# A grouped-query attention block with cached K and V: wo in longer rows, a second P buffer, a later P*V and an earlier K

## The chip, the cores and the metric

The kernel runs on one core of one Trainium2 chip. The core has five engines with queues of their own: PE (TensorE, matmuls; the trace also shows its weight loads as PEld), DVE (VectorE), ACT (ScalarE), POOL (GpSimd) and SP (SyncE, which issues nearly all transfers here). Sixteen DMA engines move data between HBM and the on-chip memory SBUF. Matmul results go to PSUM, 8 banks of 512 f32 on each of 128 partitions. The metric is the device time in microseconds of one execution; lower is better.

## The reference

32 batches, 4 query positions each, model width 1024, 32 query heads in 4 groups that share a K and V head, a cache of 2048 positions, head size 128, all bf16.

```python
q = (x @ wq).reshape(B, Sq, Hq, Dh).transpose(0, 2, 1, 3)
k = jnp.repeat(k_cache, rep, axis=1)
v = jnp.repeat(v_cache, rep, axis=1)
scores = jnp.einsum("bhqd,bhkd->bhqk", q, k) * (Dh ** -0.5)
p = softmax(scores)
o = jnp.einsum("bhqk,bhkd->bhqd", p, v)
return o.transpose(0, 2, 1, 3).reshape(B, Sq, Hq * Dh) @ wo
```

K and V of one batch are 2 MB each, wq and wo 8 MB each: some 151 MB are read once.

## The kernel before

The program is written by hand as five in-order queues. `p.op(engine, emit, waits, done)` appends an instruction with the events that it waits for; `p.dma` does the same for a transfer. Nothing reorders the queues.

**Loads.** `big` is a ring of 8 slots of 2 MB (16 KB on each of 128 partitions). First wq takes four of them; then K and V of each batch follow one another in the list `loads`: K is three batches ahead (`LEAD = 3`), so the order is K0, K1, K2, K3, V0, K4, V1 and so on, and at the end K31, V28, V29, V30, V31. SP issues them in this order (L171). Load n takes the slot of load n-8 and waits until that one has been used: a K until its four transposes are done (`("kt", b, 3)`), a V until its P*V is done (`("pv", b)`). One row of a K or V load is the 16 KB of a partition. After the last V, wo goes into the four slots that come next, in ten pieces (`WO`: seven of four heads or 1 MB, one of two, two of one head), with one row of 2 KB for each head and partition (L183).

**One batch**, i, goes through these steps:
- `kt`: DVE transposes K in four chunks of 16 positions in 32x32 blocks (L269) into one of two `KT_sb` buffers.
- `qd`: POOL lays the batch's queries out as a block diagonal over the four groups (L260), so that one matmul does all groups.
- `pe_qk`: 16 matmuls of 512 columns write the scores to `ps_s`, four PSUM banks (L281 and, with the weights held, L16). They wait for the exp of the batch before, which reads the same banks.
- `softmax_max` (DVE, L289, L290), `softmax_exp` (ACT, L294, with the sums) into `P_sb`.
- `pt`: DVE transposes P into one of two `PT_sb` (L302); `pd`: POOL copies it, group by group, into the block diagonal `PD_sb` (L314, four copies), which was cleared once. `PD_sb` is a single buffer: the copies wait for the P*V before. Batch 30 uses a second one, `PE_sb`, which is laid over a free `KT_sb` and cleared by ACT in iteration 30 (L378). Of the last batch's four copies DVE does three.
- `pe_pv`: 64 matmuls of P with V (L321) into one of four PSUM banks that are used in turn (`slot`).
- `o_evac`: ACT scales by the inverse sum into `o_sb` (L328); `pe_ot`: PE transposes it with an identity (L334); `ot_evac`: ACT writes it to `oT_sb` (L338), which is laid over `QT_sb` with the heads innermost. `o_evac` of a batch waits for the transpose of the one before, since `o_sb` is single.

**The order in iteration i** on each queue: queries i+1, half of K's transposes i+1, scores i, max i, output transpose i-3, exp i, the other half of K's transposes i+1, P's transpose i, P*V i-2 with `o_evac`, and the copies `pd` of i-1. So P*V is two batches behind the scores. After the loop come the last two P*V and what belongs to them.

**The end.** `oproj` (L349, L16) does 32 heads times two matmuls of 512 columns, each head with the wo rows of that head as moving operand and `oT_sb[:, :, h]` as weights, all into one accumulation. It waits for the last `ot_evac` and, piece by piece, for wo. Then DVE (L357) and ACT (L358) take half of the result each to `y_sb`, and SP and ACT store it (L360).

Of the kernel before, what the change touches and what calls it, by code (L numbers as in the profile page):

```python
# [78 lines left out]
def bass_standalone__gqa_block_cached__sampling_kernel(  # L79
# [21 lines left out]
    NW = 4  # L101
    LEAD = 3
    NC = D // 2
    WO = (4, 4, 4, 4, 4, 4, 4, 2, 1, 1)
# [5 lines left out]
    with ExitStack() as es:  # L110
# [8 lines left out]
        QT_sb = sbuf("QT_sb", [128, B, 2, REP, Sq, 2], BF16)  # L119
        oT_sb = QT_sb[:, :, :, :, :, :].rearrange("p b a h s w -> p (b a h s w)").rearrange("p (t h) -> p t h", h=Hq)  # L120
        QD_sb = sbuf("QD_sb", [128, 2, 2, G, 32, 2], BF16)
# [5 lines left out]
        PD_sb = sbuf("PD_sb", [128, T // 2, G, 32, 2], BF16)  # L127
        PE_sb = KT_sb[:, B % 2, :, :, :, :].rearrange("p t a r w -> p (t a r w)")
        PE_sb = PE_sb.rearrange("p (t g q w) -> p t g q w", t=T // 2, g=G, q=32)
        o_sb = sbuf("o_sb", [128, Dh], BF16)  # L130
        y_sb = sbuf("y_sb", [128, D], BF16)

# [27 lines left out]
        for b in range(B):  # L160
            loads += [("k", b + LEAD)] if b + LEAD < B else []
            loads += [("v", b)]
        slot_of = {}
        holder = {s: "w" for s in range(NW)}
        for n, (kind, b) in enumerate(loads):
            s = (NW + n) % NS
            before, holder[s], slot_of[kind, b] = holder.get(s), (kind, b), s
            waits = [] if before is None else ["qproj"] if before == "w" else [
                ("kt", before[1], NCH - 1) if before[0] == "k" else ("pv", before[1])]
            src = (k_cache if kind == "k" else v_cache)[b].rearrange("g (r t) d -> (g r) t d", r=R)  # L170
            p.dma("sp", lambda e, s=s, src=src: e.dma_start(big[:, s, :, :], src), waits, (kind, b), f"s_b{s}")  # L171
        n = len(loads)
        wo_slot = [(NW + n + c) % NS for c in range(NW)]

        def wo_at(h):
            return big[:, wo_slot[h // 8], :, :].rearrange("p t d -> p (t d)")[:, h % 8 * D:(h % 8 + 1) * D]

        h0 = 0
        for c, m in enumerate(WO):
            assert h0 // 8 == (h0 + m - 1) // 8  # L180
            kind, b = holder[wo_slot[h0 // 8]]
            dst = big[:, wo_slot[h0 // 8], :, :].rearrange("p t d -> p (t d)")[:, h0 % 8 * D:(h0 % 8 + m) * D]
            p.dma("sp", lambda e, dst=dst, h0=h0, m=m: e.dma_start(  # L183
                dst.rearrange("p (h n) -> p h n", h=m), wo[h0 * 128:(h0 + m) * 128, :].rearrange("(h p) n -> p h n", p=128)),
                [("kt", b, NCH - 1) if kind == "k" else ("pv", b)], ("wo", c), f"s_wo{c}")
            h0 += m
# [64 lines left out]

        ring_of = {}

        def qd(i):
# [50 lines left out]
        def pd_of(i):  # L305
            return PE_sb if i == B - 2 else PD_sb

        def pd(i):
            for g in range(G):
                rows = slice(32 * g, 32 * (g + 1))  # L310
                src = words(PT_sb[rows, i % 2, :, :, :].rearrange("p t q w -> p t (q w)"))
                dst = words(pd_of(i)[rows, :, g, :, :].rearrange("p t q w -> p t (q w)"))
                waits = [("pt", i)] + (["pe0"] if i == B - 2 else ["pd0"] + ([("pv", i - 2 if i == B - 1 else i - 1)] if i else []))
                p.op("dve" if i == B - 1 and g < 3 else "pool", lambda e, s=src, d=dst: e.tensor_copy(d, s),  # L314
                     waits, ("pd", i, g))

        def pe_pv(i):
            buf, waits = slot(("o", i))
            ring_of["o", i] = buf
            for t in range(T):  # L320
                p.op("pe", lambda e, t=t: e.matmul(  # L321
                    buf[:, 0:Dh], lhsT=pd_of(i)[:, t // 2, :, :, t % 2].rearrange("p g q -> p (g q)"),
                    rhs=big[:, slot_of["v", i], t, :], start=(t == 0), stop=(t == T - 1)),
                    waits + [("pd", i, g) for g in range(G)] + [("v", i)] if t == 0 else [], ("pv", i) if t == T - 1 else None)

# [5 lines left out]
        def pe_ot(i):  # L331
            buf, waits = slot(("ot", i))
            buf = ring_of["ot", i] = buf.bitcast(BF16)
            p.op("pe", lambda e: e.transpose(buf[:, 0:128], o_sb[:, :], ident[:, :]), waits + [("o", i)], ("oT", i))  # L334

        def ot_evac(i):
            buf = ring_of["ot", i]
            p.op("act", lambda e: e.activation(  # L338
                oT_sb[:, i * Sq:(i + 1) * Sq, :].rearrange("p s h -> p h s"),
                buf[:, 0:128].rearrange("p (h s) -> p h s", s=Sq), ACT.Copy),  # L340
                [("oT", i), ("qd", i)], ("ot", i))


        def oproj(c):
            for h in range(sum(WO[:c]), sum(WO[:c + 1])):
                for j in range(2):
                    out_, lhsT, rhs = ps_s[:, NC * j:NC * (j + 1)], oT_sb[:, :, h], wo_at(h)[:, NC * j:NC * (j + 1)]
                    if j == 0:
                        mm = lambda e, a=(out_, lhsT, rhs), h=h: e.matmul(  # L349
                            a[0], lhsT=a[1], rhs=a[2], start=(h == 0), stop=(h == Hq - 1), skip_group_check=True)  # L350
                    else:
                        mm = lambda e, a=(out_, lhsT, rhs), h=h: _matmul_held(
                            nc, e, *a, tile_size=(128, 128), tile_position=(0, 0), start=(h == 0), stop=(h == Hq - 1))
                    p.op("pe", mm, [("wo", c), ("ot", B - 1), ("exp", B - 1)], ("op", j) if h == Hq - 1 else None)
# [8 lines left out]
        L = B - 1  # L363
        p.at["qt_all"] = p.at["qt", 3]
        qd(0)
        kt(0, range(NCH))
        for i in range(B):
            if i < L:
                qd(i + 1)
                kt(i + 1, (0, 1))  # L370
            pe_qk(i)
            softmax_max(i)
            if i >= 3:
                pe_ot(i - 3)
                ot_evac(i - 3)
            softmax_exp(i)
            if i == L - 1:
                p.op("act", lambda e: e.memzero(words(PE_sb.rearrange("p t g q w -> p (t g q w)"))), [("qk", i)], "pe0")  # L378
            if i < L:
                kt(i + 1, (2, 3))  # L380
            pt(i)
            if i >= 2:
                pe_pv(i - 2)
                o_evac(i - 2)
            if i >= 1:
                pd(i - 1)

        pe_pv(L - 1)
        pe_ot(L - 2)
        ot_evac(L - 2)  # L390
        o_evac(L - 1)
        pd(L)
        pe_pv(L)
        pe_ot(L - 1)
        ot_evac(L - 1)
        o_evac(L)
        pe_ot(L)
# [60 lines left out]
```

## Time and profile before

| what | value |
|---|---|
| median of 5 runs | 369.34 us (369.09 to 370.71) |
| profiled execution, its own time | 369.41 us |
| its span | 367.6 us |
| PE busy | 280.5 us (76%) |
| DVE busy | 275.3 us (75%) |
| ACT busy | 123.2 us (34%) |
| POOL busy | 164.7 us (45%) |
| moved by the DMA engines | 151.90 MB, mean 413 GB/s |
| SP's loads and stores, share of 16 engines' span | 97.9% |

The span runs from the first to the last recorded instruction; the time of the execution is longer by what lies around it. Busy shares are means over stages. A slice is a fortieth of the span, 9.19 us, counted from 0 here. In lists of instructions L321 is line 321 of the kernel; "x64" means that many instructions merged; the brackets behind a line give the idle time before it on its engine and who ended it. A PE instruction is pitched closer to the next than its own duration, since matmuls are pipelined.

### The profile page before, as it was taken

To read this page: it belongs to the slowest core of one execution; us is meant where nothing else is said; L and a number is where in the kernel's file an instruction comes from. 1 tells how busy PE (TensorE), PEld (TensorE's weight loads), DVE (VectorE), ACT (ScalarE), POOL (GpSimd) and SP (SyncE) were. 2 spreads that over 40 slices of the span, in tenths; PEclk is the share of its full clock that TensorE was granted. 3 is DMA by queue.
4 is the path that set the end of the run, shared out by engine and by line. 5 is a ranking of instruction groups with operands and counts; after the bars stand their busy time and mean duration, and the time that the engine had idled before them with its cause. 6 is when DMAs were issued, how large, how long until landed. Compare 5 with 4: busy or idle time off the path is not lost.

```text
span 367.6 us, 5961 instructions
## 1 busy us (share of the span) xinstructions
PE 280.5 (76%) x2744; PEld 143.2 (39%) x2272; DVE 275.3 (75%) x273; ACT 123.2 (34%) x135; POOL 164.7 (45%) x262
## 2 busy tenths in 40 slices
PE   1982665888888888888877877787877777778796
PEld 1001001444444444444444443353544444545722
DVE  0029577999999999999999999969799888684300
ACT  1020012343333334444444444314334433456200
POOL 5002150555555555555555555555465544358100
PEclk9999668999999999999999999899899999899989
DMA  8999999999999999999999999999999999999992
GB/s 328 433 433 428 430 428 426 426 426 425 425 426 426 426 428 426 427 426 428 428 428 428 426 427 429 424 430 424 426 428 424 428 428 428 426 428 406 385 372 84
DMA packets 14506, 151.90 MB, mean 413 GB/s; under 512 B 1296, under 2 KB 1552, under 8 KB 5776
## 3 DMA queue, kind: packets, MB, share of 16 engines
q1 hardware_dynamic: 14336, 151.39, 97.9%
q8 instruction: 20, 0.33, 0.4%
q10 hardware_dynamic: 144, 0.13, 0.1%
q14 instruction: 6, 0.05, 0.0%
HBM read 151.26 MB, written 0.26 MB: 412 GB/s over the span
## 4 chain that ended last, share of the span: by engine, by line
DMA 34%; PE 31%; DVE 18%; ACT 8%; issue 7%; SPq 1%
DMA big<-in_v_cache_dram 29%; PE ps_s L16 18%; DVE mx L289 13%; ACT P_sb L294 7%; PE ps_s L281 6%; DMA big<-in_wq_dram 6%; PE ps_r L321 4%; DVE KT_sb L269 3%; PE ps_s L349 2%; DVE negmx L290 1%; DVE PD_sb L314 1%; DVE QT_sb L242 1%; DVE KT_sb L226 1%; SPq L156 0%; ACT QT_sb L338 0%
## 5 line engine op out<-in xcount | busy, mean ns | idle before, releaser
L314 POOL COPY PD_sb<-PT_sb 32x1024 f32<-32x1024 f32 x121 | 125.9, 1041 | 133.3 <-DVE KT_sb L269 67.1
L269 DVE STREAM_TRANSPOSE KT_sb<-big 128x1024 f32<-128x1024 f32 x128 | 150.7, 1217 | 6.9 <-DMA big<-in_k_cache_dram 6.8
L321 PE MATMUL ps_r<-big,PD_sb 128*128 128x128 bf16 x1984 | 120.4, 223 | 26.2 <-DMA big<-in_v_cache_dram 24.2
L321 PEld LDWEIGHTS ps_r<-big,PD_sb 128*128 128x128 bf16 x1984 | 116.2, 100 | 33.4 <-POOL QD_sb L260 26.4
L294 ACT ACTIVATE P_sb<-ps_s,negmx 128x2048 bf16<-128x2048 f32 x32 | 81.8, 2556 | 83.8 <-DVE negmx L290 83.8
L16 PE MATMUL ps_s<-KT_sb,QD_sb 128*128 128x512 bf16 x384 | 108.8, 392 | 0.0
L289 DVE TENSOR_REDUCE mx<-ps_s 128x1 f32<-128x2048 f32 x32 | 73.3, 2292 | 19.9 <-PE ps_s L16 19.5
L281 PE MATMUL ps_s<-KT_sb,QD_sb 128*128 128x512 bf16 x128 | 50.5, 394 | 45.3 <-ACT P_sb L294 39.0
L281 PEld LDWEIGHTS ps_s<-KT_sb,QD_sb 128*128 128x128 bf16 x128 | 12.7, 99 | 125.2 <-issue 74.3
L338 ACT ACTIVATE QT_sb<-ps_r 128x128 bf16<-128x128 bf16 x32 | 23.6, 737 | 105.4 <-PE ps_r L334 105.4
L302 DVE STREAM_TRANSPOSE PT_sb<-P_sb 128x1024 f32<-128x1024 f32 x32 | 39.8, 1245 | 14.8 <-ACT P_sb L294 14.8
L260 POOL COPY QD_sb<-QT_sb 32x64 f32<-32x64 f32 x128 | 29.6, 231 | 42.4 <-DVE QT_sb L242 25.5
L357 DVE CAST y_sb<-ps_s 128x512 bf16<-128x512 f32 x1 | 0.7, 692 | 21.4 <-PE ps_s L349 21.4
L226 DVE CAST KT_sb<-ps_r 128x512 bf16<-128x512 f32 x2 | 1.3, 686 | 20.2 <-PE ps_r L210 20.2
L328 ACT ACTIVATE o_sb<-ps_r,rinv 128x128 bf16<-128x128 f32 x32 | 11.9, 372 | 12.6 <-PE ps_r L321 12.5
L349 PE MATMUL ps_s<-big,QT_sb 128*128 128x512 bf16 x32 | 13.2, 412 | 0.9 <-ACT QT_sb L338 0.9
L16 PE MATMUL ps_s<-big,QT_sb 128*128 128x512 bf16 x32 | 13.1, 411 | 0.0
L334 PEld LDWEIGHTS ps_r<-ident,o_sb 128*128 128x128 bf16 x32 | 3.1, 96 | 23.4 <-issue 21.6
L16 PE MATMUL ps_s<-big,P_sb 128*128 128x512 bf16 x32 | 9.5, 426 | 0.0
L349 PEld LDWEIGHTS ps_s<-big,QT_sb 128*128 128x128 bf16 x32 | 4.7, 147 | 11.4 <-issue 11.2
L228 ACT ACTIVATE KT_sb<-ps_r 128x512 bf16<-128x512 f32 x2 | 1.1, 595 | 23.6 <-PE ps_r L16 23.6
L210 PEld LDWEIGHTS ps_r<-big,P_sb 128*128 128x128 bf16 x8 | 0.8, 104 | 19.8 <-issue 14.9
(30 smaller groups left out, 69.3 us busy)
## 6 DMA issues: line engine op xcount, KB each, us to landing
big<-in_k_cache_dram SPq DMA_DIRECT2D x32, 2048.0 KB, 26.8
big<-in_v_cache_dram SPq DMA_DIRECT2D x32, 2048.0 KB, 31.4
big<-in_wq_dram SPq DMA_DIRECT2D x4, 2048.0 KB, 14.0
big<-in_wo_dram SPq DMA_DIRECT2D x7, 1024.0 KB, 19.0
big<-in_wo_dram SPq DMA_DIRECT2D x1, 512.0 KB, 12.8
big<-in_wo_dram SPq DMA_DIRECT2D x2, 256.0 KB, 10.4
P_sb<-in_x_dram SPq DMA_DIRECT2D x1, 256.0 KB, 2.6
out_dram<-y_sb SPq DMA_DIRECT2D x1, 128.0 KB, 1.8
```

Source lines behind the costliest of these rows:

```text
L16: return eng.add_instruction(mybir.InstMatmult(name=nc.get_next_instruction_name(), engine=eng.engine, start_tensor_calc=start, stop_tenso ...
L260: p.op("pool", lambda e, s=src, d=dst: e.tensor_copy(d, s), waits if g == 0 else [], ("qd", i) if g == G - 1 else None)
L269: p.op("dve", lambda e, s=src, d=dst: e.transpose(d, s), waits, ("kt", i, c))
L281: mm = lambda e, a_=(out_, lhsT, rhs), f=first, l=last: e.matmul(a_[0], lhsT=a_[1], rhs=a_[2], start=f, stop=l, skip_group_check=True)
L289: p.op("dve", lambda e: e.tensor_reduce(mx[:, i % 4:i % 4 + 1], ps_s[:, :], AX.X, ALU.max), [("qk", i)], ("mx", i))
L294: p.op("act", lambda e: e.activation(P_sb[:, :, :, :].rearrange("p t r w -> p t w r"), ps_s[:, :].rearrange("p (t w r) -> p t w r", w=2, r=R),
L302: p.op("dve", lambda e: e.transpose(dst, src), [("exp", i)] + ([("pd", i - 2, G - 1)] if i > 1 else []), ("pt", i))
L314: p.op("dve" if i == B - 1 and g < 3 else "pool", lambda e, s=src, d=dst: e.tensor_copy(d, s), waits, ("pd", i, g))
L321: p.op("pe", lambda e, t=t: e.matmul(buf[:, 0:Dh], lhsT=pd_of(i)[:, t // 2, :, :, t % 2].rearrange("p g q -> p (g q)"), rhs=big[:, slot_of ...
L328: p.op("act", lambda e: e.activation(o_sb[:, :], buf[:, 0:Dh], ACT.Copy, scale=rinv[:, i % 4:i % 4 + 1]), [("pv", i), ("rinv", i)] + ([("o ...
L338: p.op("act", lambda e: e.activation(oT_sb[:, i * Sq:(i + 1) * Sq, :].rearrange("p s h -> p h s"), buf[:, 0:128].rearrange("p (h s) -> p h ...
L349: mm = lambda e, a=(out_, lhsT, rhs), h=h: e.matmul(a[0], lhsT=a[1], rhs=a[2], start=(h == 0), stop=(h == Hq - 1), skip_group_check=True)
```

## The change

Three things are changed together.

1. wo is read so that one row holds two consecutive rows of the matrix, 4 KB; the last two pieces of one head stay at 2 KB. With that a partition holds other rows of wo than before (rows 2p and 2p+1 of a block of 256 for partition p), so the output must be transposed to fit: even and odd elements of `o_sb` apart, even and odd heads on different halves of the partitions, by four plain matmuls of 64 by 64 in place of one transpose. `oT_sb` becomes a tensor of its own, with the 128 tokens innermost, read by the projection without a stride. `y_sb` is laid over `P_sb`.
2. At batch 9 (`SPB`) one slot leaves the ring and becomes `PF_sb`, a second P buffer; from the load of K12 on, the ring has seven slots. Odd batches after 9 use `PF_sb`, even ones `PD_sb`, so the copies of a batch wait for the P*V two batches before. ACT clears the buffer in iteration 9. The buffer over `KT_sb` and the three copies on DVE in the last batch are gone: POOL does all copies.
3. P*V goes from two to three batches behind: in iterations 12 to 15 (`SW`, `EASE`) 48 of its 64 matmuls are issued, so that it falls back by a quarter of a batch each time. From batch 17 (`SL`) on, K is four batches ahead in the list of loads instead of three: at 17 two K loads are issued ahead of V17. The order at the end is K31, V27, V28, V29, V30, V31.

```diff
+    SL = 17
+    SW = 12
+    SPB = 9
+    EASE = 4
-        oT_sb = QT_sb[:, :, :, :, :, :].rearrange("p b a h s w -> p (b a h s w)").rearrange("p (t h) -> p t h", h=Hq)
+        oT_sb = sbuf("oT_sb", [128, Hq // 2, 2, NT], BF16)
-        PE_sb = KT_sb[:, B % 2, :, :, :, :].rearrange("p t a r w -> p (t a r w)")
-        y_sb = sbuf("y_sb", [128, D], BF16)
+        y_sb = P_flat[:, D:2 * D]
-            loads += [("k", b + LEAD)] if b + LEAD < B else []
-            loads += [("v", b)]
+            ahead = [b + LEAD] if b < SL else [b + LEAD, b + LEAD + 1] if b == SL else [b + LEAD + 1]
+            loads += [("k", a) for a in ahead if a < B] + [("v", b)]
+        n_pd = loads.index(("k", SPB + LEAD))
+        spare = (NW + n_pd) % NS
+        pd_holder = loads[n_pd - NS]
+        def ring_slot(n):
+            if n < n_pd:
+                return (NW + n) % NS
+            return (spare + 1 + (n - n_pd) % (NS - 1)) % NS
...
+        wo_v = wo.rearrange("(h p e) n -> p h (e n)", p=128, e=2)
...
+            if m > 1:
+                dst = wo_at(h0, m).rearrange("p (h n) -> p h n", n=2 * D)
+                src = wo_v[:, h0 // 2:(h0 + m) // 2, :]
+            else:
+                dst, src = wo_at(h0, 1), wo_v[:, h0 // 2, h0 % 2 * D:(h0 % 2 + 1) * D]
...
         def pd_of(i):
-            return PE_sb if i == B - 2 else PD_sb
+            return PF_sb if i > SPB and i % 2 else PD_sb
...
-                p.op("dve" if i == B - 1 and g < 3 else "pool", lambda e, s=src, d=dst: e.tensor_copy(d, s),
-                     waits, ("pd", i, g))
+                p.op("pool", lambda e, s=src, d=dst: e.tensor_copy(d, s), [("pt", i), free], ("pd", i, g))
...
-            p.op("pe", lambda e: e.transpose(buf[:, 0:128], o_sb[:, :], ident[:, :]), waits + [("o", i)], ("oT", i))
+            for e_ in range(2):
+                for u in range(2):
+                    out_ = buf[64 * u:64 * (u + 1), 64 * e_:64 * (e_ + 1)]
+                    lhsT = o_sb.rearrange("p (d e) -> p e d", e=2)[:, e_, :]
+                    rhs = ident.rearrange("p (h u s) -> p u h s", u=2, s=Sq)[:, u, :, :]
+                    p.op("pe", lambda e, a=(out_, lhsT, rhs): e.matmul(a[0], lhsT=a[1], rhs=a[2], start=True, stop=True),
+                         waits + [("o", i)] if e_ == u == 0 else [], ("oT", i) if e_ == u == 1 else None)
...
+        def pv_until(i):
+            less = min(max(i - SW + 1, 0), EASE) * (T // EASE)
+            return max((i - 1) * T - less, 0)
...
-        for i in range(B):
+        for i in range(B + 2):
+            upto = pv_until(i) if i < B else (i - 2) * T if i == B else B * T
...
+            if i == SPB:
+                p.op("act", lambda e: e.memzero(words(PF_sb.rearrange("p t g q w -> p (t g q w)"))),
+                     [("kt", pd_holder[1], NCH - 1) if pd_holder[0] == "k" else ("pv", pd_holder[1])], "pf0")
...
+            for k in range(done, upto):
+                pe_pv(k // T, k % T)
+                if k % T == T - 1:
...
+                    o_evac(k // T)
+            done = upto
```

## The prediction

> **What bounds the kernel now.** I read the slices of the page first, then the stretches of the end, then the chain of waits, then the instructions in order of time. Every time below is on the clock of the profiled execution: span 367.6 us, its own time 369.41, so 1.81 us lie around the span. The median of the runs is 369.34, 0.07 less.
>
> ```profile
> PEclk9999668999999999999999999899899999899989
> DMA  8999999999999999999999999999999999999992
> GB/s 328 433 433 428 430 428 426 426 426 425 425 426 426 426 428 426 427 426 428 428 428 428 426 427 429 424 430 424 426 428 424 428 428 428 426 428 406 385 372 84
> ```
>
> The 16 transfer engines are never idle before the last slice, so the stream of loads bounds the kernel. But from slice 37 on they are just as busy at 406, 385 and 372 GB/s: there wo is loaded, in 2 KB rows, where K and V come in 16 KB rows. So there is room in the rate of the last 8 MB, and in what follows the stream. The stretches of the end (columns: busy time and count of PE, PEld, DVE, ACT, POOL, then granted clock, DMA share, GB/s):
>
> ```profile
> 253.53:256.95 3.42, 1.46 (x16) 0.65 (x12) 3.17 (x4) 0.73 (x1) 2.15 (x6) 1.00 1.01 431
> 301.32:304.73 3.41, 1.51 (x8) 0.19 (x2) 3.33 (x3) 0.73 (x1) 3.04 (x7) 1.00 1.02 432
> 345.69:349.11 3.42, 1.59 (x23) 1.18 (x20) 0.00 (x0) 1.55 (x3) 0.00 (x0) 1.00 1.05 387
> 349.11:352.52 3.41, 3.41 (x10) 0.69 (x5) 0.00 (x0) 0.00 (x0) 0.00 (x0) 0.50 1.06 389
> ```
>
> The fourth row is the start of the output projection, at half clock. The chain that ended last shows what it waited for (start, length, what):
>
> ```profile
> 289.55 36.68 DMA big<-in_v_cache_dram
> 326.37 3.73 PE ps_r L321 x64
> ...
> 342.96 3.75 PE ps_r L321 x64
> 347.04 0.60 ACT o_sb L328
> 347.95 0.73 ACT QT_sb L338
> 348.82 0.40 PE ps_s L349
> ...
> 364.54 0.60 ACT y_sb L358
> ```
>
> Batch 28's V lands at 326.2; from there P*V of 28, the scores of 31, P*V of 29, 30, 31 follow one another on PE. The projection runs 348.82 to 364.33 without a wait: 9 matmuls at 427 ns, then 55 at 215.5. The last wo piece (issued 352.2, 10.2 us to landing) is there at 362.4, over a microsecond before PE comes to it. So the end is set by PE's late start and its half clock, with the stream 1.3 us behind as the next limit (362.44 + 0.15 + two matmuls 0.43 = 363.0). From 364.33 to the end of the span 3.27 us go to the evacuation and the store.
>
> **Part 1, wo by 4 KB rows.** By the trace's landing records, a 2 MB K or V load lands 4.893 us after the one before: 8 packets of 16 KB on each engine, 611.6 ns each. A 1 MB wo piece follows in 2.70 us: 32 packets of 2 KB, 84.4 ns each. The line through both is 9.0 ns a packet plus 36.8 ns a KB, so 4 KB costs 159.6 ns and 1 MB 16 x 159.6 = 2.55 us. Seven pieces of 1 MB and one of 0.5 MB change, two of 256 KB stay: 7.5 x 0.146 = 1.1 us. Bounds: nothing, if 4 KB costs twice 2 KB; 7.5 x (2.70 - 2.45) = 1.9 if it moves at the 16 KB rate. [...] The rows disagree (385 against 428 GB/s with both sides busy all the time), so I take 1.1: last piece at 361.35, stream-bound PE end 361.95.
>
> The layout that goes with it: four plain 64x64 matmuls instead of one 128x128 transpose of o_sb (217 ns). Price between 0.1 us (four times half of a 55 ns pitch) and 0.9 (four times 217); I take 0.3. In the loop 32 times 0.1 to 0.7 more lies in PE's waits for V and for the exp (24.2 and 39.0 us idle); without that cover it would cost some 3 us. Their evacuation reads f32 and writes runs of four elements, where L338 (737 ns) wrote single elements; L328 takes 372 for as many f32 elements. I take 0.37, bounds 0.37 and 0.74. The projection's weights become contiguous; L349's PEld of 147 ns lies under a 215 ns matmul already: nothing.
>
> **Part 2, the second P buffer and seven ring slots.** A load waits for the release of the slot seven loads back. The queue shows what there is to spare:
>
> ```profile
> SPq L171 <- DVE KT_sb L269: 245.8, 30, 11.0
> ```
>
> SP itself waits most of the time, which is harmless while the engines have queued work. The tightest new wait is V of batch 9: issued at 113.92 before; now it takes the slot of K9, whose last transpose is done in iteration 8, near 122.4 (where the next K went out before). SP is in order, so K13 stands behind it. V9 landed at 137.2 and K12's first engines are free at 130.5: 8 us to spare. Before, K7 went out at 68.97 with its turn at about 76.6, 7.6 us, and the slice there shows 426 GB/s. An iteration takes 8.92 us and two loads 9.79, so 0.87 us are gained with every batch. Cost zero; without the cover each microsecond of lateness is a microsecond of the end. The memset of the buffer (3.61 us on ACT, L378) moves from iteration 30 to 9, between two exps 6.3 us apart, beside 1.1 us of evacuations: hidden. Three copies of the last batch go from DVE (2.85 us beside one on POOL) to POOL (four, 4.33 us).
>
> **Part 3, three behind, K four ahead.** In batches 12 to 15 each iteration issues 48 of 64 P*V matmuls; the iteration is set by scores 3.6, max 2.3, exp 2.6 through ps_s, not by them: nothing. K four ahead moves no bytes; SP issues the same loads, but K31 lands one load earlier and V27 where K31 did, at 321.3 (issued 288.0, 33.3 us). V28 to V31 keep their places: 326.2, 331.1, 336.0, 340.9 (V31 issued 307.6, 33.3 us).
>
> The end then, step by step:
> - P*V 27: 321.5, pitch 3.57 (326.37 to 329.94 before). Scores 31: 325.05, pitch 3.47, K31's transposes being over by 324. Before they began at 329.94.
> - Transpose 27: 0.3. P*V 28: 328.85 to 332.6.
> - POOL is next. P of 30 uses the buffer of 28, P of 31 that of 29, and POOL is in order:
>
> ```profile
> 330.23 4.33 POOL L314 COPY PD_sb<-PT_sb 32x1024 f32<-32x1024 f32 x4 [4.19 <-PE ps_r L321]
> 334.71 4.33 POOL L314 COPY KT_sb<-PT_sb 32x1024 f32<-32x1024 f32 x4 [0.16 <-POOL PD_sb L314]
> 340.08 1.56 POOL L314 COPY PD_sb<-PT_sb 32x1024 f32<-32x1024 f32 x1 [1.04 <-DVE rinv L303]
> ```
>
>   The copies of 30: 332.8 to 337.1, of 31: 337.3 to 341.6 (its transpose is ready at 335.3, P*V 29 done at 336.4). P*V 30 lies beside them, 337.3 to 341.0.
> - P*V 31: V is there at 340.9, P at 341.6, so 341.7 to 345.45. Before: 342.96 to 346.71.
> - Transpose 30 0.3, then o_sb at 345.95 for 0.6, transpose 31, evacuation 0.37 to 347.4: the projection starts at 347.5, 1.3 us earlier (347.9 with the dearer evacuation).
>
> **The clock.** Unthrottled the projection takes 64 x 0.2155 = 13.8 us, at half clock for one window 15.5. Of the three 3.4 us windows shown, the one with 1.51 us of PE kept its clock and the one with 1.59 lost it, so busy time alone doesn't decide. [...] By the rule PE ends at 347.5 + 13.8 = 361.3 and the stream decides, 361.95; with the clock lost as in the row, at 363.0.
>
> **The sum.** 361.95 + 3.27 = 365.2, + 1.81 = 367.0, against 369.41; less the 0.07 to the median, 367.0. It is a gain of 2.4 us, 0.65%.
>
> **Rivals.**
> - The clock drops again: 347.5 + 15.5 + 3.27 + 1.81 = 368.1; with the dear evacuation and slower small matmuls 368.7. For it: the row at 349.11, in all likelihood in every run, as their times agree. [...]
> - The change doesn't do what it says: 4 KB rows land as 2 KB rows do (363.0 + 5.08 = 368.1), and the two copies on POOL run longer, so that the projection starts at 348.8 at half clock: 369.4. For it: the tail now hangs on POOL, 8.7 us without slack.
> - Slower: the seven-slot ring lets the stream run dry at V9. It decides from the point where V9's issue comes more than 8 us later than I have it, one iteration (8.92 us) being enough; the stream ends later by all that is beyond 8, and 2.4 us of that eat the gain. If each of the following V loads slips by an iteration while the slack grows by 0.87 a batch, about 4 us are lost: 371. Against it: K7's 7.6 us sufficed, and SP waits 11 us at a time without a dip in GB/s.
>
> **How the numbers follow.** No change here means within 0.3%, 368.2 to 370.4, about what the runs (369.09 to 370.71) can tell apart. Forecast 0.52; clock lost 0.25; no effect 0.13; ring dry 0.10. The forecast's own range is 366.1 (4 KB at the 16 KB rate) to 368.1. The clock case lies to both sides of 368.2 (0.17 and 0.08), no effect mostly in the band (0.05 faster, 0.07, 0.01). Faster 0.72, same 0.16, slower 0.12. The range leaves out the ring case and the ends: 366.1 to 369.6.
>
> **What would show it.** Right: the last full slices above 390 GB/s; 1 MB wo pieces landing 2.55 us apart; P*V 31 beginning near 341.7 behind POOL; projection from about 347.5 with granted clock 1.0; PE waiting for the last wo piece. Wrong: a slice under 420 GB/s between 110 and 340 us (ring), half clock after 347 (gate), wo pieces 2.70 apart (rows), or P*V 31 later than 343 (POOL).

## The result, and the profile after

The changed kernel takes 367.37 us in the median (27 executions, 367.19 to 368.25); the kernel before, run beside it on the same chips, 369.35 (48 executions). The ratio is 0.9935 with a 95% interval of 0.9922 to 0.9947: 0.65% faster, 2.0 us by the medians. The profiled execution took 367.14 us with a span of 365.3, against 369.41 and 367.6. Two executions of the experiments below, one of E9 (994 us) and one of E11 (382.9 us), ran in a slow state and are left out of their medians.

The slices of the page of the changed kernel (granted clock in tenths, busy share of the transfer engines, GB/s):

```profile
PEclk9998678999999999998889999999999999999999
DMA  8999999999999999999999999999999999999993
GB/s 325 431 434 427 429 429 427 427 429 428 428 427 431 423 427 424 423 431 425 429 429 429 425 424 422 427 431 429 427 431 420 427 425 425 431 423 423 406 405 122
```

Where the last two full slices showed 385 and 372 GB/s they show 406 and 405: that is wo in 4 KB rows. By the landing records the 1 MB pieces follow one another in 2.55 us instead of 2.70, and the last piece lands at 361.08 instead of 362.44. The clock is at 9 in every slice from 21 on (counted from 0). In slices 18 to 20, where P*V falls back, it is a little lower, and the stream doesn't feel it (425 to 429 GB/s).

The chain that ended last, changed kernel (start, length, what):

```profile
295.63 25.42 DMA big<-in_v_cache_dram
321.09 3.75 PE ps_r L341 x64
...
332.29 1.04 POOL PD_sb L332
...
336.68 3.52 PE ps_r L341 x60
340.20 18.34 DMA big<-in_wo_dram
362.25 0.60 ACT P_sb L383
```

The chain no longer goes through `o_sb`, its transpose and the projection's first matmul. It passes through a transfer of wo, issued at 340.20 and landed at 358.54; most of that time it stands behind earlier pieces, which land 2.55 us apart. The projection has become the follower of the stream.

The end in order of time, changed kernel (start, length, then idle time before and who ended it):

```profile
332.29 4.33 POOL L332 COPY PD_sb<-PT_sb 32x1024 f32<-32x1024 f32 x4 [3.00 <-PE ps_r L341]
336.78 4.33 POOL L332 COPY big<-PT_sb 32x1024 f32<-32x1024 f32 x4 [0.16 <-POOL PD_sb L332]
341.17 3.75 PE L341 MATMUL ps_r<-big 128*128 128x128 bf16 x64 [0.56 <-POOL big L332]
...
345.31 0.36 ACT L348 ACTIVATE o_sb<-ps_r,rinv 128x128 bf16<-128x128 f32 x1
345.73 0.25 PE L359 MATMUL ps_r<-ident,o_sb 128*64 128x64 bf16 x4 [0.63 <-ACT o_sb L348]
346.02 0.28 ACT L364 ACTIVATE oT_sb<-ps_r 128x128 bf16<-128x128 f32 x1 [0.35 <-PE ps_r L359]
346.44 0.38 PE L374 MATMUL ps_s<-big,oT_sb 128*128 128x512 bf16 x1 [0.46 <-ACT oT_sb L364]
...
358.58 0.39 PE L374 MATMUL ps_s<-big,oT_sb 128*128 128x512 bf16 x1 [0.57 <-DMA big<-in_wo_dram]
...
362.03 0.69 DVE L382 CAST P_sb<-ps_s 128x512 bf16<-128x512 f32 x1 [27.23 <-PE ps_s L374]
```

P*V of 31 begins at 341.17 instead of 342.96, behind POOL's copies. From there to the projection it is 5.27 us instead of 5.86, so the projection starts 2.4 us earlier, at 346.44. But it ends only 2.3 us earlier although it no longer loses 1.7 us to the clock (granted 1.00 from 346.44 to 362.00, where before had 0.50 from 349.11 to 352.52). At 358.58 it waits for the seventh of the 1 MB pieces (landed 358.54), and the 16 matmuls that are left then (its own eight and those of the three small pieces), 3.45 us, give the end at 362.03.

### The profile page after: what moved, and what is told of

It is laid out like the page before. It is cut to its first block, busy times and chain, and to the rows that moved or that the text cites. A ratio compares the mean times of both kernels' runs of the same rounds, so it can differ in the third digit from the quotient of the medians.

```text
span 365.3 us, 6105 instructions
## 1 busy us (share of the span) xinstructions
PE 284.5 (78%) x2840; PEld 138.6 (38%) x2368; DVE 271.7 (74%) x270; ACT 107.6 (29%) x135; POOL 167.3 (46%) x265
## 4 chain that ended last, share of the span: by engine, by line
PE 37%; DVE 22%; ACT 19%; DMA 18%; issue 2%; POOL 2%; SPq 0%; POOLq 0%
PE ps_s L16 24%; ACT P_sb L311 18%; DVE mx L306 17%; PE ps_s L298 9%; DMA big<-in_v_cache_dram 7%; DMA big<-in_wq_dram 6%; DMA big<-in_wo_dram 5%; PE ps_r L341 4%; DVE KT_sb L286 2%; POOL PD_sb L332 2%; DVE negmx L307 1%; DVE QT_sb L258 1%; DVE KT_sb L242 1%; PE ps_s L374 1%; SPq L158 0%
## 5 line engine op out<-in xcount | busy, mean ns | idle before, releaser
L332 POOL COPY PD_sb<-PT_sb 32x1024 f32<-32x1024 f32 x84 | 87.0, 1036 | 91.7 <-PE ps_r L341 64.0
L16 PE MATMUL ps_s<-KT_sb,QD_sb 128*128 128x512 bf16 x384 | 112.1, 402 | 0.0
L298 PE MATMUL ps_s<-KT_sb,QD_sb 128*128 128x512 bf16 x128 | 51.6, 403 | 58.7 <-ACT P_sb L311 50.3
L341 PE MATMUL ps_r<-big,PD_sb 128*128 128x128 bf16 x1344 | 79.0, 219 | 3.2 <-DMA big<-in_v_cache_dram 2.5
L341 PEld LDWEIGHTS ps_r<-big,PD_sb 128*128 128x128 bf16 x1344 | 75.3, 98 | 6.0 <-DMA big<-in_v_cache_dram 2.6
L332 POOL COPY big<-PT_sb 32x1024 f32<-32x1024 f32 x44 | 45.6, 1036 | 39.7 <-PE ps_r L341 33.0
L341 PE MATMUL ps_r<-big 128*128 128x128 bf16 x704 | 41.4, 219 | 3.3 <-DMA big<-in_v_cache_dram 2.7
L364 ACT ACTIVATE oT_sb<-ps_r 128x128 bf16<-128x128 f32 x32 | 8.9, 278 | 116.1 <-PE ps_r L359 116.1
L341 PEld LDWEIGHTS ps_r<-big 128*128 128x128 bf16 x704 | 39.4, 98 | 3.9 <-DMA big<-in_v_cache_dram 2.9
L359 PEld LDWEIGHTS ps_r<-ident,o_sb 128*64 128x64 bf16 x128 | 4.6, 109 | 31.2 <-issue 29.0
L374 PE MATMUL ps_s<-big,oT_sb 128*128 128x512 bf16 x32 | 12.2, 380 | 1.7 <-DMA big<-in_wo_dram 1.2
L16 PE MATMUL ps_s<-big,oT_sb 128*128 128x512 bf16 x32 | 12.1, 379 | 0.0
```

The costliest lines, as they stand in the source:

```text
L16: return eng.add_instruction(mybir.InstMatmult(name=nc.get_next_instruction_name(), engine=eng.engine, start_tensor_calc=start, stop_tenso ...
L298: mm = lambda e, a_=(out_, lhsT, rhs), f=first, l=last: e.matmul(a_[0], lhsT=a_[1], rhs=a_[2], start=f, stop=l, skip_group_check=True)
L332: p.op("pool", lambda e, s=src, d=dst: e.tensor_copy(d, s), [("pt", i), free], ("pd", i, g))
L341: p.op("pe", lambda e: e.matmul(buf[:, 0:Dh], lhsT=pd_of(i)[:, t // 2, :, :, t % 2].rearrange("p g q -> p (g q)"), rhs=big[:, slot_of["v", ...
L364: p.op("act", lambda e: e.activation(oT_sb[:, :, :, i * Sq:(i + 1) * Sq].rearrange("p h e s -> p e h s"), buf[:, 0:128].rearrange("p (e h ...
L374: mm = lambda e, a=(out_, lhsT, rhs), h=h: e.matmul(a[0], lhsT=a[1], rhs=a[2], start=(h == 0), stop=(h == Hq - 1), skip_group_check=True)
```

## The experiments

Two questions were open. Which part of the change brings the gain? And does the projection's time depend on the half clock at its start, and what goes ahead of that? The theory on record: rows 1.1 us, the clock kept, and a projection that starts 1.3 us earlier thanks to the order of parts 2 and 3. The rivals: the rows alone, the layout alone, or the order alone carry it. Each kernel was run in five rounds beside the kernel before. The medians of before on the three occasions were 369.39 (E1 to E4), 370.71 (E5 to E8) and 370.26 (E9 to E12); its executions lie in clusters near 369.3 and 370.9, so a ratio over 20 to 32 of them is uncertain by some 0.2 to 0.3%. The ratio uses the runs of before on the same occasion; differences of medians between runs of different occasions are less certain.

| run | kernel | us | ratio to before, 95% |
|---|---|---|---|
| E1 | before, plain matmul for the transpose | 369.19 | 0.9991 (0.9966 to 1.0016) |
| E2 | before with part 1 alone | 367.69 | 0.9938 (0.9914 to 0.9963) |
| E3 | after, wo in 2 KB rows | 368.24 | 0.9954 (0.9933 to 0.9975) |
| E4 | after, K three ahead throughout | 371.14 | 1.0038 (1.0017 to 1.0059) |
| E5 | after, P*V two behind throughout | 374.54 | 1.0127 (1.0095 to 1.0160) |
| E6 | after without part 3 | 370.17 | 1.0007 (0.9986 to 1.0029) |
| E7 | before with part 1's layout, 2 KB rows | 368.41 | 0.9947 (0.9929 to 0.9965) |
| E8 | after, last `o_sb` step four times | 368.31 | 0.9961 (0.9939 to 0.9982) |
| E9 | before, PE kept busy ahead of the projection | 368.81 | 0.9970 (0.9949 to 0.9991) |
| E10 | after, wo in 8 KB rows | 367.37 | 0.9927 (0.9900 to 0.9954) |
| E11 | after, ring of seven from batch 3 | 367.61 | 0.9935 (0.9911 to 0.9959) |
| E12 | after again | 367.30 | 0.9926 (0.9900 to 0.9953) |

### E1: a plain matmul for the transpose

```diff
-            p.op("pe", lambda e: e.transpose(buf[:, 0:128], o_sb[:, :], ident[:, :]), waits + [("o", i)], ("oT", i))
+            p.op("pe", lambda e: e.matmul(buf[:, 0:128], lhsT=o_sb[:, :], rhs=ident[:, :], start=True, stop=True),
+                 waits + [("o", i)], ("oT", i))
```

> The kernel before, with one edit: the transpose of o_sb is an ordinary 128x128 matmul with the identity, and its evacuation reads f32 in place of bf16. [...]

E1 took 369.19 us, no different from before. Stretches of the end of this run (columns: busy time and count of PE, PEld, DVE, ACT, POOL, then granted clock, transfer share, GB/s), and two lines in order of time:

```profile
345.70:349.11 3.41, 1.59 (x20) 1.05 (x15) 0.00 (x0) 1.55 (x3) 0.00 (x0) 1.00 1.05 386
349.11:352.53 3.42, 3.42 (x10) 0.67 (x4) 0.00 (x0) 0.00 (x0) 0.00 (x0) 0.50 1.05 386
```

```profile
347.73 0.72 ACT L339 ACTIVATE QT_sb<-ps_r 128x128 bf16<-128x128 f32 x1 [0.32 <-PE ps_r L334]
348.60 0.41 PE L350 MATMUL ps_s<-big,QT_sb 128*128 128x512 bf16 x1 [0.91 <-ACT QT_sb L339]
```

The 3.41 us ahead of the half clock hold 1.59 us of PE as before, now all of it in ordinary matmuls, and the granted clock still drops to 0.50 at 349.11. So ordinary matmuls in place of these two transposes did not keep the clock. The second view answers another question: the evacuation reads f32 here and still takes 0.72 us, so what makes it dear is the writing of single elements (64 bytes apart), not the bf16 source.

### E2 and E7: part 1 alone, and its layout alone

E2 is before with the whole of part 1 (rows, layout, four small matmuls, `y_sb` over `P_sb`). E7 is the same, but each wo piece of more than one head comes as two transfers of 2 KB rows:

```diff
+            free = [("kt", b, NCH - 1) if kind == "k" else ("pv", b)]
+            if m > 1:
+                for x in range(2):
+                    p.dma("sp", lambda e, dst=dst, src=src, x=x: e.dma_start(
+                        dst[:, :, x * D:(x + 1) * D], src[:, :, x * D:(x + 1) * D]), free, ("wo", c) if x else ("wo_", c), f"s_wo{c}")
...
```

> The kernel before with part 1 alone: wo by 4 KB rows, the four 64x64 matmuls, oT_sb as a tensor of its own. Ring, second P buffer, order of P*V and K as before. Theory: the last wo piece lands at about 361.2, the projection starts near 348.4 at full clock and takes 13.8, so PE ends at 362.2: 367.3 us, the whole gain of the change to within 0.4 us. Rival (the gain comes from the new order of K and P*V, which brings the projection forward): with the old order the projection starts at 348.4 and loses the clock, 363.9, 369.0 us.

> The kernel before with the layout of part 1 alone: four 64x64 matmuls, oT_sb apart with tokens innermost, wo to the same places, but every piece of more than one head in two transfers of 2 KB rows. Theory: the cheaper evacuations (0.28 and 0.36 us in place of 0.73 and 0.59 at the end) shorten PE's gap before the projection from 2.3 to 1.6 us, so the clock stays at 1.0, and the stream with its last piece near 362.3 decides: 368.3 us, 1.1 below before. Rival (all of part 1 is the row size): 369.3.

E2 took 367.69 us and E7 368.41. Part 1 alone gives 0.9938, which is not to be told from the whole change; the layout without the longer rows gives 0.9947. The intervals of the two overlap. Six of E2's nine executions lie between 367.27 and 367.75, below all of E7's (368.13 to 368.62); the other three take 368.48 to 369.21. By the medians, which come from two occasions, some 1.0 us of 1.7 is the layout's and 0.7 the rows', and the profiles below give the same split. In E7, in order of time, and then the stretch that holds the gap (columns as in E1):

```profile
347.96 0.36 ACT L337 ACTIVATE o_sb<-ps_r,rinv 128x128 bf16<-128x128 f32 x1
348.37 0.25 PE L348 MATMUL ps_r<-ident,o_sb 128*64 128x64 bf16 x4 [0.63 <-ACT o_sb L337]
348.67 0.28 ACT L353 ACTIVATE oT_sb<-ps_r 128x128 bf16<-128x128 f32 x1 [0.35 <-PE ps_r L348]
349.09 0.38 PE L363 MATMUL ps_s<-big,oT_sb 128*128 128x512 bf16 x1 [0.46 <-ACT oT_sb L353]
```

```profile
347.39:350.80 3.41, 2.32 (x20) 0.77 (x13) 0.00 (x0) 0.81 (x3) 0.00 (x0) 1.00 1.05 387
```

and in E2:

```profile
343.60 3.75 PE L325 MATMUL ps_r<-big,PD_sb 128*128 128x128 bf16 x64 [0.60 <-DVE PD_sb L318]
...
348.87 0.38 PE L358 MATMUL ps_s<-big,oT_sb 128*128 128x512 bf16 x1 [0.46 <-ACT oT_sb L348]
```

The evacuation in runs of four takes 0.28 us instead of 0.73, and `o_evac` ahead of it 0.36 instead of 0.60, since it no longer queues behind a dear evacuation on ACT. From P*V of 31 to the projection it is 5.27 us (348.87 - 343.60). The projection starts no earlier than before, as P*V of 31 began later in these two profiles (343.6 and 343.8): V of 27 landed at 316.32 and 316.59 there, against 315.02 in the profile of before, and what follows on PE came later with it. But the projection runs at full clock throughout (matmul records of 0.38 us, against up to 0.63 at half clock in before), and in E7 the 3.41 us from 347.39, which hold the whole gap, have 2.32 us of PE and a granted clock of 1.00. So the final evacuation starts at 363.34 in E7 and at 362.67 in E2, against 364.33 in the kernel before. The gain of part 1 is the shorter gap, which keeps the clock, and then the rows.

### E3 and E10: the size of the rows

E3 is after with the two transfers of E7's diff. E10 makes rows of 8 KB:

```diff
-        wo_v = wo.rearrange("(h p e) n -> p h (e n)", p=128, e=2)
+        wo_v = wo.rearrange("(h p e) n -> p h (e n)", p=128, e=4)
...
-            for e_ in range(2):
-                for u in range(2):
+            for e_ in range(4):
+                for u in range(4):
...
```

> The changed kernel, with every wo piece of more than one head loaded as two transfers of 2 KB rows into the same places; all else is the same. Theory (the stream sets the end, and the row size sets its last 8 MB): pieces of 1 MB land 2.70 us apart again, the last one 1.1 to 1.2 us later, near 362.2, and all of it is paid: 368.5 us. Rival (the gain is PE's earlier start and full clock): PE has slack behind the stream the other way round, nothing is lost, 367.4. Rival (2 KB and 4 KB rows move alike): pieces land as far apart as in the changed kernel, 367.4.

> The changed kernel taken one step on: four wo rows to a partition, 8 KB rows (the pieces of two and one heads 4 and 2 KB), and so sixteen 32x32 matmuls for each batch's transpose. By the line through the two measured row sizes 8 KB costs 310 ns a packet, 2.48 us for 1 MB in place of 2.55: 7 pieces give 0.5 us, the last piece lands near 360.6. Each transpose takes some 0.4 us more on PE, three of them at the end: the projection starts near 347.4 and ends near 361.2 by PE and by the stream alike. Theory: 366.9 us, 0.5 below the changed kernel. Rival (sixteen matmuls cost 55 ns and more each, 0.9 us a batch, and lengthen the gap): 368 or more.

E3 took 368.24 us. Its 1 MB pieces land 2.70 us apart again, the last at 362.20, although its projection starts at 347.39, early enough. Its page and order of time:

```profile
GB/s 334 435 433 429 426 429 424 427 426 427 425 427 427 424 427 427 426 427 427 427 424 429 426 425 428 426 429 426 426 427 426 427 427 426 429 426 410 387 384 119
```

```profile
359.67 0.39 PE L379 MATMUL ps_s<-big,oT_sb 128*128 128x512 bf16 x1 [0.63 <-DMA big<-in_wo_dram]
```

The seventh piece releases PE at 359.67 instead of 358.58: the rows are worth 1.1 us at that point in the profiles and 0.9 us in the medians, and no execution of E3 (368.15 to 368.81) is as short as the longest of E12 (367.46). E10 took 367.37 us beside 367.30 for the unchanged kernel after. The line through 2 KB and 16 KB rows (9.0 ns a packet and 36.8 ns a KB) holds, with the KB as 1000 bytes: 8 KB took some 309 ns where it says 310, pieces of 1 MB came 2.47 us apart, the last one landed at 360.86. Its 16 small matmuls take 0.32 us. In its profile, E10's fastest execution (366.91 us), the projection began at 347.78, still early enough, and the seventh piece (landed 358.33) sets the end: the final evacuation starts at 361.82, 0.2 us before that of the kernel after, since the last V landed 0.3 us later. The 0.5 us that the rows save on the pieces do not show in the medians; why is open.

### E4, E5 and E6: the order of parts 2 and 3

```diff
 # E4
-    SL = 17
+    SL = 99
 # E5
-    SW = 12
+    SW = 99
 # E6: both
```

> The changed kernel with K three batches ahead to the end (P*V still three behind). K31 lands one load later, near 321.0, its second pair of transposes is over near 326, scores 31 start near 326.0 instead of 324.7, the projection near 347.7 instead of 346.4. Theory (the stream sets the end): the projection still ends before the last wo piece, 367.4 us, no difference. Rival (PE's chain sets the end): 1.3 us later, 368.7.

> The changed kernel with P*V two batches behind to the end (K still four ahead from batch 17). Scores 31 come after P*V 28 again, near 329.7; the last P is transposed near 340.2, POOL's four copies end near 344.7, the projection starts near 350.0 instead of 346.4. Theory (a later P*V takes POOL's copies of the last batch off the end): PE ends at 350.0 + 13.8 = 363.8, 1.6 us after the changed kernel: 369.0 us. Rival (the stream hides it): 367.4.

> The changed kernel without part 3: K three ahead and P*V two behind all through; wo rows, layout, second P buffer and seven-slot ring stay. With P*V two behind, K31 lands at 321 and is not waited for until 329.7, so K's place in the list does nothing: as the run with P*V two behind, 369.0 us, and 1.3 us slower than part 1 alone (367.7), since POOL makes the last batch's four copies (4.33 us) where DVE took three of them (2.85 us). Rival (the seven slots or the second buffer cost nothing and gain nothing): 367.7.

All three missed. Within parts 1 and 2 the four combinations are: neither half of part 3, 370.17; K four ahead alone, 374.54; P*V three behind alone, 371.14; both, 367.37. K alone costs 4.4 us, the later P*V alone 1.0 (an amount that the intervals of E4 and E6, from two occasions, just fail to separate), and together they save 2.8.

E4 in order of time:

```profile
321.11 2.37 DVE L286 STREAM_TRANSPOSE KT_sb<-big 128x1024 f32<-128x1024 f32 x2 [2.37 <-DMA big<-in_k_cache_dram]
323.40 2.25 DVE L306 TENSOR_REDUCE mx<-ps_s 128x1 f32<-128x2048 f32 x1
325.88 2.53 ACT L311 ACTIVATE P_sb<-ps_s,negmx 128x2048 bf16<-128x2048 f32 x1 [4.19 <-DVE negmx L307]
328.60 0.58 PE L298 MATMUL ps_s<-KT_sb,QD_sb 128*128 128x512 bf16 x1 [3.54 <-ACT P_sb L311]
```

With K three ahead K31 lands at 321.0. Its first transposes stand on DVE ahead of the maximum of 30, which so begins at 323.40; the exp of 30 and, through `ps_s`, the scores of 31 follow. PE is empty for 3.54 us, loses its clock (granted 0.50 from 327.45 to 334.28, matmuls of 0.58 to 0.63 us), P*V of 28 slips to 335.12 and the projection to 353.12. All of wo was there at 361.29, but the final evacuation starts only at 366.92.

E5 in order of time:

```profile
311.41 4.99 PE L341 MATMUL ps_r<-big,PD_sb 128*128 128x128 bf16 x64 [3.07 <-DMA big<-in_v_cache_dram]
...
334.10 0.38 PE L298 MATMUL ps_s<-KT_sb,QD_sb 128*128 128x512 bf16 x1 [1.42 <-ACT P_sb L311]
...
344.24 4.32 POOL L332 COPY big<-PT_sb 32x1024 f32<-32x1024 f32 x4 [4.62 <-DVE rinv L320]
348.62 5.16 PE L341 MATMUL ps_r<-big 128*128 128x128 bf16 x64 [3.27 <-POOL big L332]
```

Here each V is one load later, but P*V wants it one iteration earlier. P*V of 26 stands on PE ahead of the scores of 29, waits 3.07 us for V and then takes 4.99 us instead of 3.73 to 3.75 (the granted clock from 300 to 340 us is 0.96 in the mean). The scores of 29, 30 and 31 follow from there at 316.23, 325.19 and 334.10 (324.67 in the kernel after), and the projection begins at 355.30.

E6 in order of time:

```profile
339.94 4.32 POOL L332 COPY big<-PT_sb 32x1024 f32<-32x1024 f32 x4 [5.48 <-DVE rinv L320]
344.32 5.38 PE L341 MATMUL ps_r<-big 128*128 128x128 bf16 x64 [3.26 <-POOL big L332]
```

All four copies of batch 31 lie on POOL and end at 344.26; in E2, where DVE does three of them, they began 0.75 us later and ended at 343.5. PE waits 3.26 us, and P*V of 31 itself then runs mostly at half clock (granted 0.50 from 345.60 to 349.00), 5.38 us instead of 3.75. Together 2.35 us: the projection starts at 351.22 (E2: 348.87), and the times differ by 2.5. So part 2 alone gives away the gain of part 1, and part 3 gets it back. With both halves of part 3 the scores of 31 are computed while P*V would be waiting for V, and POOL has its last copies done by 341.1, 0.4 us after the last V (340.70).

### E8 and E9: the length of the gap

E8 repeats the last `o_sb` step three times more in the kernel after, which lengthens the gap ahead of the projection by 1.2 us. E9 gives PE six extra matmuls of 512 columns in the two waits ahead of the projection in the kernel before:

```diff
 # E8
+            prev = [("pv", i), ("rinv", i)] + ([("oT", i - 1)] if i else [])
+            for x in range(4 if i == B - 1 else 1):
+                done = ("o", i) if i < B - 1 or x == 3 else ("ox", x)
+                p.op("act", lambda e: e.activation(o_sb[:, :], buf[:, 0:Dh], ACT.Copy, scale=rinv[:, i % 4:i % 4 + 1]), prev, done)
+                prev = [done]
 # E9
+        def keep_busy(n):
+            for _ in range(n):
+                p.op("pe", lambda e: e.matmul(ps_s[:, 0:NC], lhsT=ident[:, :], rhs=P_flat[:, 0:NC],
+                                              start=True, stop=True, skip_group_check=True), [("exp", L)])
...
+        keep_busy(3)
         pe_ot(L)
+        keep_busy(3)
```

> The changed kernel with the scaling of the last batch's o_sb done four times over (same values), so that PE idles about 1.2 us longer before the projection, 2.8 us in place of 1.6. Nothing else is touched. The projection starts near 347.7; at full clock it would end at 361.5, still before the last wo piece lets it. [...] Rival (the gap does not matter to the clock): 367.5 throughout.

> The kernel before with six extra matmuls of 512 columns (into ps_s, which the projection then overwrites) in the two waits between the last P*V and the projection, three before the last transpose and three after it: they fill waits of 0.9 us each with 0.65 us. Nothing is computed from them. [...]

E8 took 368.31 us, spread over 367.31 to 370.0: three of twelve executions take up to 367.63, four 368.17 to 368.34, and five 369.19 to 370.0, above the range of the kernel after. So the longer gap does cost time in most of them. The profiled one was the fastest. Its stretches:

```profile
165.50:168.91 3.41, 3.41 (x10) 0.29 (x2) 3.10 (x4) 0.00 (x0) 0.69 (x4) 0.50 0.98 418
175.74:179.15 3.41, 3.41 (x9) 0.34 (x3) 3.41 (x4) 0.09 (x1) 2.09 (x6) 0.50 1.00 428
342.99:346.41 3.42, 2.89 (x53) 2.67 (x50) 0.00 (x0) 0.49 (x2) 0.00 (x0) 1.00 1.03 410
346.41:349.82 3.41, 1.65 (x11) 0.53 (x8) 0.00 (x0) 1.42 (x5) 0.00 (x0) 1.00 1.02 405
345.00:348.41 3.41, 1.14 (x21) 0.82 (x19) 0.00 (x0) 1.91 (x6) 0.00 (x0) 1.00 1.02 404
```

The first two rows are half-clock stretches in mid-kernel. Their starts are 10.24 us apart, three times 3.413. In the profile of before, those after 200 us last 3.41 us each and start at 236.47, 256.95, 314.97 and 349.11: 6, 17 and 10 such steps apart. Carried on from 165.50 with that step, an estimate, an edge falls at 346.41, inside the gap. So the gap is shared between two stretches in step with the half-clock ones, with 2.89 and 1.65 us of PE, and the clock is kept (1.00 in both), while a stretch that happened to begin at 345.00 would have held 1.14. That in the slower executions of E8 the stretches fell the other way is argued and not shown, as no profile of such an execution was taken. For it: the mean granted clock, which is on record for each execution, is 0.963 to 0.967 in the three fastest and 0.949 to 0.957 in the five slowest, by an estimate from these figures one to four half-clock stretches more. Against it: two of the four in between have 0.963, like two of the fastest; and one stretch at half clock costs 1.7 us (15.5 against 13.8 for the projection), which takes the profiled execution to 369.0, where the slowest five took up to 370.0.

E9 took 368.81 us, 0.3% below before. Five of its eleven executions lie between 368.3 and 368.63; but three are still near 369.3 and two above 370. The profiled one took 369.17. Two lines of its order of time:

```profile
326.18 5.36 PE L321 MATMUL ps_r<-big,PD_sb 128*128 128x128 bf16 x64 [3.98 <-DMA big<-in_v_cache_dram]
...
350.25 0.42 PE L349 MATMUL ps_s<-big,QT_sb 128*128 128x512 bf16 x1 [0.26 <-ACT QT_sb L338]
```

With the gap filled, the projection, though it starts at 350.25, runs at full clock (final evacuation from 364.09, 13.84 later, where before took 15.5): with the matmuls in it the gap cost no clock. (This does not tell one long standstill from too little work: the extra matmuls mend both.) The same profile shows a second such place: P*V of 28, which waited 3.98 us for V, takes 5.36 us, as long as that of 31 in E6 at half clock (5.38), instead of the 3.73 of before, and all that follows is 1.4 us later. So this profile could gain little.

### E11 and E12: the ring, and after once more

```diff
-    SPB = 9
+    SPB = 3
```

> The changed kernel with the slot leaving the ring at batch 3 instead of 9, when compute is behind the loads: V3 waits for K3's last transpose in iteration 2, near 68.9, and its turn on the transfer engines comes near 72, three microseconds later, against eight at batch 9. Theory (a load needs little more than a microsecond from issue to first packet): the stream still never runs dry, 367.4 us. Rival (a queue of fewer than two loads starves): the slices near 70 us fall below 420 GB/s and each microsecond is paid at the end, 368.5 or more.

> The changed kernel once more, beside the others on the same chip: 367.4 us, for a comparison with the 8 KB rows.

E11 took 367.61 us (0.9935). Its slices:

```profile
GB/s 328 430 434 428 427 428 425 428 425 427 426 428 430 427 425 427 427 428 427 430 427 427 427 427 425 427 427 423 427 428 425 430 428 427 430 425 417 406 401 111
```

No slice from the second to the 36th is under 423 GB/s: even with the ring cut six batches earlier, with less slack, the stream does not run dry. (In the profiles of before and after the first load moves its first bytes 1.0 us after its issue: 0.73 to 1.73 and 0.74 to 1.74.) V of 3 went out 8.1 us later than in the kernel before (66.47 against 58.40) and landed at the same time (78.47 against 78.42). E12 gave 367.30 (367.2 to 367.46).

## Why the prediction was right

The time (367.0, measured 367.37), the cause of the end (a stream that PE waits for) and most steps hold. The reason for the clock is shown by no run, the one for where the gain comes from does not hold, and part of the agreement is luck: PE began the projection 1.1 us earlier than forecast, which does not show in the time only because the stream decides, and in the stream's own sum two errors cancel.

- **Rows: right.** 159.6 ns a packet was worked out from 2 KB and 16 KB rows; 1 MB came in the 2.55 us of the forecast, and E3 shows 0.9 us for it. Had 2 KB and 4 KB rows moved alike, E3 would have equalled after; it was 0.87 us slower.
- **The steps of the end: right within 0.55 us**, each a little early: scores 31 at 324.67 (325.05 forecast), P*V 28 at 328.42 (328.85), POOL's copies 332.29 and 336.78 (332.8, 337.3), P*V 31 at 341.17 (341.7).
- **From P*V 31 to the projection: mis-sized.** 5.8 us in the forecast, 5.27 measured, so the projection began at 346.44 and not 347.5. `o_evac` was put at 0.6, as L328's last row shows; it is 0.36, because that row was queueing behind the dear evacuation. The new evacuation is 0.28 (0.37 taken), the small matmuls 0.25 (0.3 taken).
- **The stream-bound end: right by two errors that cancel.** The forecast let the last piece decide, its landing plus 0.15 and two matmuls: 361.08 + 0.58 = 361.66 by the measured landing. What decided was the seventh 1 MB piece and the 16 matmuls behind it, 362.03. The last piece came 0.27 earlier than forecast (361.35), which made up for most of it: 361.95 forecast, 362.03 measured, and from there to the end of the span 3.27 us as before. The sign named for it, PE waiting for the last piece, did not come: PE waited for the fifth, sixth and seventh, and no longer for the last three.
- **The clock: right result, but no run shows its reason.** The 361.3 of the forecast takes the whole projection at full clock; that held (granted 1.00 from 346.44 to 362.00), but the rule that the sentence goes by is shown by no run: it was the author's assumption. What the runs show: in E1, with ordinary matmuls for the two transposes, the 3.41 us ahead of the projection hold 1.59 us of PE and the clock drops all the same. In after the gap ahead of the projection is 1.6 us of near idleness (344.84 to 346.44) instead of 2.1 to 2.3, and the 3.41 us that hold it have 2.33 us of PE; E7 keeps the clock with the layout alone, E9 with the gap filled. That stretch of after, in step with its half-clock stretches, and then the two stretches that follow the prediction's second and first rows in the kernel before:

```profile
344.41:347.83 3.42, 2.33 (x24) 1.00 (x18) 0.00 (x0) 0.81 (x3) 0.00 (x0) 1.00 1.03 410
```

```profile
304.73:308.14 3.41, 2.77 (x50) 2.80 (x51) 2.96 (x5) 2.63 (x2) 0.20 (x1) 1.00 0.99 423
256.95:260.36 3.41, 3.41 (x36) 3.41 (x34) 3.02 (x3) 2.60 (x2) 0.00 (x0) 0.50 1.00 428
```

  So recorded busy time does not order the stretches: those with 1.46 and 1.59 us were followed by half clock, that with 1.51 was not. A record is longer than its pitch to the next: 380 ns against 215.5 for 512 columns, 220 against 55.8 for 128. With each matmul and transpose counted by its pitch from its start (64 columns in proportion), an estimate, the three hold 1.28, 1.21 and 1.34 us, that of E1 1.2, and those around the gap in after and E7 1.8 and 1.9. In the profiles of before and after together, counted in this way over the 169 full-clock stretches of 3.41 us after 60 us that lie in step with the half-clock ones, the seven that were followed by half clock hold at most 1.28 us and the others at least 1.29. So in these two profiles the estimated work in a stretch goes with the clock of the next one, and the longest pause does not: pauses of up to 1.9 us kept the clock (301.32 to 304.73 in before), and the stretch at 345.69, which lost it, has none over 0.92. What sets the clock is not shown beyond that.
- **Where the gain comes from: not as the sum suggested.** The sum let part 3 start the projection 1.3 us earlier and part 1 take the clock and the rows. E2 shows that part 1 alone brings 367.69: at full clock, its final evacuation starts at 362.67. Parts 2 and 3 then start the projection 2.4 us earlier (346.44 against 348.87), but wo is not there, and the final evacuation comes only 0.64 earlier. Their share is 0.3 us by the medians, not to be told from nothing. That they make the time steadier (367.19 to 368.25 against 367.27 to 369.21) is suggested, with 9 executions on one side; the slack behind the stream, which E2 lacks, would be the reason (see the point on the lost clock).
- **"Part 3: nothing" and "cost zero" for the ring: right for both together.** What the text did not price is each without the other. E6 shows that moving DVE's three copies to POOL, which the forecast passed over as 2.85 us becoming 4.33, costs 2.5 us without part 3; E4 and E5 that neither half of part 3 alone brings the gain.
- **The rival of a ring run dry** is refuted by after's slices and by E11. V of 9 went out at 121.35, where some 122.4 was forecast, and landed at 137.05 (137.24 before).
- **The rival of a lost clock** did not occur in the profile. After's narrow spread does not show that it never does: its executions near 367.3 have mean granted clocks from 0.953 to 0.967, in no order with their times. Half clock for one stretch at the start of the projection would be hidden: PE would come to the seventh piece at 346.44 + 48 x 0.2155 + 1.7 = 358.5 us, an estimate, and that piece lands at 358.54. So, by this profile, the time of the kernel after no longer depends on the step about the clock.
- **The chances** given for the single cases add up to 0.74, 0.15 and 0.11, and not to the 0.72, 0.16 and 0.12 stated. Nothing rests on it.

## What to carry to other kernels

When a stream bounds a kernel, cost every edit of its tail twice, once from the engine's side and once from the landing of each late piece with the work still behind it; the later of the two is the gain's limit, and an earlier start beyond it is worth nothing. Changes of an order that move loads and their consumers by one step belong together: judge them in all combinations, since here one half alone was 4.4 us slower, the other no faster, and both together 2.8 faster. A short wait ahead of dense matmuls can cost more than its length: here waits of 2.1 to 2.3 us were followed by half clock, which cost another 1.7 us. So look at the granted clock behind such a wait, and shorten it (here by writing the evacuation in runs of four), or start so early that a stream hides the loss.

## What the runs showed of the hardware that was not expected

- ACT's 128x128 evacuation took 0.73 us when writing single bf16 elements 64 bytes apart, from bf16 or from f32, and 0.28 us in runs of four, less than the 0.36 of the contiguous one with a scale.
- Four 64x64 matmuls took 0.25 us from first to last, sixteen of 32x32 0.32: little more than one 128x128 transpose (0.22).
- Half-clock stretches lasted 3.41 us (before after 200 us, E1, E8), one in E4 twice that (327.45 to 334.28), and started whole multiples of 3.41 us apart (before: 236.47, 256.95, 314.97, 349.11; E8: 165.50 and 175.74). A wait of 2.1 to 2.3 us ahead of the projection was followed by one in before and E1, and one of 3.26 us in P*V in E6 (granted 0.50); after a wait of 3.98 us in E9 P*V took as long as there (5.36 us against 5.38). A gap of 2.8 us in E8 went free (granted 1.00); the edge carried on from 165.50, an estimate, falls inside it.
